# Placing the queries of 16 attention units with stride-one columns, and copying the first layer's result on one engine

## The chip, the cores and the metric

The kernel runs on one core of a Trainium2 chip. The metric is device time in microseconds (us). TensorE (PE, with its weight loads as PEld) multiplies, VectorE (DVE), ScalarE (ACT) and GpSimd (POOL) do elementwise work, SyncE (SP) issues every DMA of this kernel, in one queue.

## What is computed

Chunked local attention, then two feed-forward layers. Four batches, eight heads, 768 positions, head size 64. For each chunk of 32 queries the keys are 8 memory keys and the window from 16 positions before the chunk to 8 behind it, 64 in all where the sequence doesn't cut it:

```python
scores = scale * np.matmul(q_c, k_full.transpose(0, 1, 3, 2))
a = softmax(scores)                       # over the 64 keys
out[:, :, c_start:c_end] = np.matmul(a, v_full)
...
x = out as (3072, 512)                    # heads side by side
x = leaky_relu(x @ w_in, 0.01) @ w_out    # 512 -> 2048 -> 512
return (x @ w_a) * (x @ w_b) @ w_out2     # 512 -> 1536 -> 512
```

All inputs and outputs are float32.

## The kernel before

The 3072 tokens form six blocks of 512 (`bi` 0 to 5); each block is four attention units of 128 tokens, so there are 24 units. While TensorE works on the first feed-forward layer of block `bi`, the attention of block `bi + 1` is put between its steps. A step `f` of a block is one of the 16 slices of the layer's 2048 hidden columns: `mm1` (12 matmuls, lines 303 to 305) into a PSUM bank, a Prelu by ScalarE (line 383), a rounding copy by ScalarE (`gh`, line 320), a subtraction (`gl`, line 321), and two steps later `mm2` (12 matmuls, lines 398 to 402) into the four accumulators `acc[bi][e]` of the block. At a block's end the accumulators are copied to SBUF tiles `x2` (lines 410 and 412) and written to DRAM (line 413). The four PSUM buffers `a` of the accumulators are the same for all blocks, so the next block's first `mm2` waits for these copies. The tiles `x2` share three buffers (tag `z`).

Unit `u` of block `bi + 1` is spread over the steps of block `bi`: scores at step `f` (2, 5, 8, 11; in block 0 5, 8, 11, 14), softmax at `f` and `f + 1`, transposes by VectorE at `f + 2`, the product with the values (`a_pv`, line 276) and its copy out (`a_out`) at `f + 3`.

The scores of a unit are 16 products of 128x64 weights, the queries, with 64 columns of keys (line 202); in the trace they are 32 weight loads and 32 matmuls. The 64 query columns hold two heads: partitions 0 to 63 hold one head in columns 0 to 31 and zeros in the others, partitions 64 to 127 the other head in columns 32 to 63. The tile is laid out `[partition, column, o]` with 16 products `o`, so the 64 columns of one product lie 16 floats apart. Two such tiles `Q` are used in turn; the zeros are written once at the start (lines 158 to 160), and two DMAs for each unit write the queries into their halves (lines 173 and 174). `load_qk(u)` loads the queries up to unit `u + 2`, right behind the scores of `u`.

The values of `a_pv` are weights of the same 128x64 shape, `v[:, i:i + 64]`, with their columns next to each other.

In blocks 0 to 4 ScalarE, VectorE and GpSimd also prepare the weights of the later layer (`prep_steps`, lines 471 to 515): load raw words, join, round, subtract, store. ScalarE and VectorE execute in the order that the planner of the language gave them. After the last block the second layer runs (lines 660 to 741).

Of the kernel before, what the change touches and what calls it, by code (L numbers as in the profile page):

```python
# [7 lines left out]
F32 = mybir.dt.float32  # L8
# [6 lines left out]
P = 128  # L15
B, H, S, D = 4, 8, 768, 64
CH, LEFT, RIGHT, NMEM = 32, 16, 8, 8
# [3 lines left out]
NU = B * UPB  # L21
# [10 lines left out]
def kernel(  # L32
# [10 lines left out]
    nc = tc.nc  # L43
# [11 lines left out]
    tp = ctx.enter_context(tc.tile_pool(name="tp", bufs=4, side="right"))  # L55
# [96 lines left out]
    Q = [ap_.tile([P, 2 * CH, 16], F32, tag=f"q{i}", name=f"q{i}", bufs=1) for i in range(2)]  # L152
# [16 lines left out]
    def q_load(upto):  # L169
        while loaded[0] < min(upto, NU):  # L170
            u = loaded[0]
            qb = Q[u % 2]
            nc.sync.dma_start(out=qb[0:64, 0:CH, :], in_=q_l[u, 0:64])
            nc.sync.dma_start(out=qb[64:128, CH:2 * CH, :], in_=q_l[u, 64:128])
            loaded[0] += 1

    def k_load(upto):
        while loaded[1] < min(upto, 2 * NU):
            u, cp = divmod(loaded[1], 2)
            t = ap_.tile([P, 512], F32, tag="k", name="k")  # L180
            nc.sync.dma_start(out=t, in_=k_l[u, cp])
            kt[u, cp] = t
            loaded[1] += 1
# [8 lines left out]

    def a_scores(u):
        qb = Q[u % 2]
        s = ps_s.tile([P, 8, 64], F32, tag="s", name="s")
        for cp in range(2):
            k = kt.pop((u, cp))
            for hp in range(4):
                for cpar in range(2):
                    o = (2 * cp + cpar) * 4 + hp  # L200
                    r = (cpar * 4 + hp) * 64
                    nc.tensor.matmul(  # L202
                        s[64 * cpar:64 * cpar + 64, cp * 4 + hp, :],
                        qb[:, :, o],
                        k[:, r:r + 64],
                        start=True, stop=True,
                    )
        st[u] = s
# [123 lines left out]

    x_tiles(("x", 0))
    q_load(1)
    k_load(2)
    q_load(2)
    k_load(4)
    nc.sync.dma_start(out=ident, in_=id_l)
    v_load(4)
    W1.load(1)  # L340
    k1 = kt[1, 1]
    a_scores(0)
    a_scores(1)

    warm = ps_a.tile([P, TB], F32, tag="a", name="warm")
    with tc.high_priority(offset=-100000):
        for _ in range(8):
            nc.tensor.matmul(
                warm[:, 0:128], k1[:, 0:128], k1[:, 0:128], start=True, stop=True
            )  # L350
    q_load(4)
    k_load(8)
    W1.load(4)
# [14 lines left out]
    W1.split(1, nc.vector)  # L368
    a_out(1, ("x", 0), UT)
    a_scores(2)  # L370
    a_soft1(2)

# [13 lines left out]
    def mm2(bi, parts, g):  # L386
        if bi not in acc:
            acc[bi] = [ps_a.tile([P, TB], F32, tag="a", name="a") for _ in range(KC)]
        gh, gl = g
        for o, n, f in parts:  # L390
            slot = wslot[f, 1]
            t = slice(o, o + n)
            for e in range(KC):
                ps = acc[bi][e][:, t]
                c = slice(e * P, e * P + P)

                kw = dict(skip_group_check=n < TB)
                nc.tensor.matmul(  # L398
                    ps, slot[:, 1, c], gh[:, t], start=f == 0 and o == 0, stop=False, **kw
                )  # L400
                nc.tensor.matmul(ps, slot[:, 0, c], gl[:, t], start=False, stop=False, **kw)  # L401
                nc.tensor.matmul(  # L402
                    ps, slot[:, 0, c], gh[:, t], start=False, stop=f == NF1 - 1, **kw
                )
            if f == NF1 - 1:
                for e in range(KC):
                    ps = acc[bi][e][:, t]
                    y = tp.tile([P, TB], F32, tag="z", name="x2", bufs=3)
                    if e % 2:
                        nc.vector.tensor_copy(y[:, t], ps)  # L410
                    else:
                        nc.scalar.copy(y[:, t], ps)
                    nc.sync.dma_start(out=x2d[bi][:, e, t], in_=y[:, t])

    HALF, LEAD = TB // 2, 3
# [12 lines left out]
    def at(bi, f, fn, *args):  # L428
        beside.setdefault((bi, f), []).append(lambda: fn(*args))
# [22 lines left out]
    for bi in range(NB3 - 1):  # L452
        for k, f in enumerate([5, 8, 11, 14] if bi == 0 else [2, 5, 8, 11]):
            u = (bi + 1) * (TB // UT) + k
            at(bi, f, a_scores, u)
            at(bi, f, load_qk, u)
            at(bi, f, a_soft1, u)
            at(bi, f + 1, a_soft2, u)
            at(bi, f + 2, a_turn, u)
            at(bi, f + 3, a_pv, u, ps_s, "s")  # L460
            at(bi, f + 3, load_v, u)
            at(bi, f + 3, a_out, u, ("x", bi + 1), k * UT)
# [125 lines left out]
    for n, (bi, f, parts) in enumerate(items):  # L588
# [16 lines left out]
        if len(behind) > LAG:  # L605
            mm2(*behind.pop(0))
# [31 lines left out]
    for it in behind:  # L638
        mm2(*it)
# [191 lines left out]
```

## Time and profile before

| | us |
|---|---|
| median of three runs | 1192.63 (1191.24 to 1194.59) |
| profiled execution | 1194.71 |
| its span, first to last instruction | 1192.9 |
| TensorE matmul busy | 1158.3 (97%) |
| TensorE weight loads busy | 974.7 (82%) |
| VectorE busy | 681.2 (57%) |
| ScalarE busy | 383.2 (32%) |
| GpSimd busy | 109.6 (9%) |

Busy times are those of the engine's own instructions. Weight loads run beside matmuls. A busy TensorE may still be paced by its weight loads, since matmuls overlap each other in the records.

### The profile page before, as it was taken

To read this page: it belongs to the slowest core of one execution; us is meant where nothing else is said; L and a number is where in the kernel's file an instruction comes from. 1 tells how busy PE (TensorE), PEld (TensorE's weight loads), DVE (VectorE), ACT (ScalarE), POOL (GpSimd) and SP (SyncE) were. 2 spreads that over 40 slices of the span, in tenths; PEclk is the share of its full clock that TensorE was granted. 3 is DMA by queue.
4 is the path that set the end of the run, shared out by engine and by line. 5 is a ranking of instruction groups with operands and counts; after the bars stand their busy time and mean duration, and the time that the engine had idled before them with its cause. 6 is when DMAs were issued, how large, how long until landed. Compare 5 with 4: busy or idle time off the path is not lost.

```text
span 1192.9 us, 16632 instructions
## 1 busy us (share of the span) xinstructions
PE 1158.3 (97%) x6632; PEld 974.7 (82%) x6632; DVE 681.2 (57%) x1246; ACT 383.2 (32%) x642; POOL 109.6 (9%) x77
## 2 busy tenths in 40 slices
PE   5799999999998999999999999999999999999998
PEld 4799988878886888888888888888888888888887
DVE  5979876978768694644511543457433456433444
ACT  3735343444334343223422222233122233122210
POOL 1421211231222230000000000000000000000000
PEclk9899999999998999999999999999999999999999
DMA  9867788879697887434435733537453535453512
GB/s 333 295 220 246 248 293 298 310 268 321 253 337 254 292 297 258 142 107 159 159 106 220 265 124 124 194 124 291 159 203 124 194 124 220 159 203 124 194 62 106
DMA packets 63821, 250.71 MB, mean 210 GB/s; under 512 B 7424, under 2 KB 8832, under 8 KB 56832
## 3 DMA queue, kind: packets, MB, share of 16 engines
q1 hardware_dynamic: 63744, 249.66, 58.8%
q8 instruction: 52, 0.85, 0.3%
q14 instruction: 25, 0.20, 0.0%
HBM read 200.34 MB, written 49.28 MB: 209 GB/s over the span
## 4 chain that ended last, share of the span: by engine, by line
PE 81%; DVE 10%; DMA 3%; POOL 2%; issue 2%; ACT 1%; SPq 0%; DVEq 0%; ACTq 0%; POOLq 0%
PE o L727 5%; PE o L729 5%; PE o L728 5%; PE h L303 5%; PE a L398 5%; PE a L401 5%; PE a L402 5%; PE h L304 5%; PE h L305 5%; PE A L660 4%; PE A L662 4%; PE A L661 4%; PE C L660 3%; PE C L662 3%; PE C L661 3%; PE s L202 3%
## 5 line engine op out<-in xcount | busy, mean ns | idle before, releaser
L303 PE MATMUL h<-xh,w 128*128 128x512 f32 (+1 forms) x448 | 165.2, 369 | 5.5 <-DVE w L94 5.5
L398 PE MATMUL a<-gh,w 128*128 128x512 f32 (+1 forms) x448 | 162.4, 362 | 8.3 <-DVE x L410 7.1
L401 PE MATMUL a<-gl,w 128*128 128x512 f32 (+1 forms) x448 | 161.9, 361 | 5.3 <-POOL gl L321 5.3
L304 PE MATMUL h<-xl,w 128*128 128x512 f32 (+1 forms) x448 | 161.8, 361 | 0.0
L305 PE MATMUL h<-xh,w 128*128 128x512 f32 (+1 forms) x448 | 161.7, 361 | 0.0
L402 PE MATMUL a<-gh,w 128*128 128x512 f32 (+1 forms) x448 | 161.6, 361 | 0.0
L321 DVE TENSOR_TENSOR gl<-g,gh 128x512 fp32r<-128x512 f32 x80 | 61.9, 776 | 102.2 <-ACT gh L320 101.5
L727 PE MATMUL o<-w,cl 128*128 128x512 f32 x288 | 112.1, 389 | 0.0
L729 PE MATMUL o<-w,ch 128*128 128x512 f32 x288 | 112.0, 389 | 0.0
L728 PE MATMUL o<-w,ch 128*128 128x512 f32 x288 | 112.0, 389 | 0.0
L383 ACT ACTIVATE g<-h 128x512 f32<-128x512 f32 (+1 forms) x99 | 57.5, 580 | 157.1 <-PE h L305 157.1
L398 PEld LDWEIGHTS a<-gh,w 128*128 128x128 f32 x448 | 85.4, 191 | 23.0 <-DVE x L410 8.6
L303 PEld LDWEIGHTS h<-xh,w 128*128 128x128 f32 x448 | 85.1, 190 | 19.5 <-issue 5.8
L401 PEld LDWEIGHTS a<-gl,w 128*128 128x128 f32 x448 | 85.5, 191 | 18.0 <-POOL gl L321 5.5
L246 DVE STREAM_TRANSPOSE pt<-p 32x128 f32<-32x128 f32 x320 | 96.8, 302 | 5.3
L402 PEld LDWEIGHTS a<-gh,w 128*128 128x128 f32 x448 | 85.6, 191 | 12.6
L305 PEld LDWEIGHTS h<-xh,w 128*128 128x128 f32 x448 | 85.1, 190 | 13.0
L304 PEld LDWEIGHTS h<-xl,w 128*128 128x128 f32 x448 | 85.3, 190 | 12.0
L674 ACT COPY u<-A 128x512 f32<-128x512 f32 x72 | 42.3, 587 | 143.6 <-PE A L662 143.6
L682 DVE TENSOR_TENSOR ga<-u,C 128x512 f32<-128x512 f32 x36 | 24.8, 688 | 105.1 <-ACT u L674 75.9
L660 PE MATMUL A<-ch,wab 128*128 128x512 f32 x216 | 84.1, 389 | 0.0
L661 PE MATMUL A<-cl,wab 128*128 128x512 f32 x216 | 84.1, 389 | 0.0
(94 smaller groups left out, 1970.7 us busy)
## 6 DMA issues: line engine op xcount, KB each, us to landing
wab<-wab SPq DMA_DIRECT2D x36, 1792.0 KB, 7.3
w<-wod SPq DMA_DIRECT2D x116, 512.0 KB, 4.7
raw<-w SPq DMA_DIRECT2D x68, 512.0 KB, 6.3
wab<-pw SPq DMA_DIRECT2D x12, 1792.0 KB, 6.8
k<-kl SPq DMA_DIRECT2D x48, 256.0 KB, 4.9
v<-vl SPq DMA_DIRECT2D x48, 256.0 KB, 5.2
wod<-w SPq DMA_DIRECT2D x16, 512.0 KB, 5.5
q<-ql SPq DMA_DIRECT2D x48, 128.0 KB, 5.1
```

The costliest lines, as they stand in the source:

```text
L246: nc.vector.transpose(out=pt[o0:o0 + 32, :, 2 * cpar + hpar, hpx, :], in_=p[i0:i0 + 32, hpx::2, 32 * b:32 * b + 32],)
L303: nc.tensor.matmul(ps, w[1], x[0], start=first, stop=False)
L304: nc.tensor.matmul(ps, w[0], x[1], start=False, stop=False)
L305: nc.tensor.matmul(ps, w[0], x[0], start=False, stop=last)
L398: nc.tensor.matmul(ps, slot[:, 1, c], gh[:, t], start=f == 0 and o == 0, stop=False, **kw)
L401: nc.tensor.matmul(ps, slot[:, 0, c], gl[:, t], start=False, stop=False, **kw)
L402: nc.tensor.matmul(ps, slot[:, 0, c], gh[:, t], start=False, stop=f == NF1 - 1, **kw)
L660: nc.tensor.matmul(ps, w[:, 1, i, c], hi[:, kc], start=first and kc == 0, stop=False, **kw)
L661: nc.tensor.matmul(ps, w[:, 0, i, c], lo[:, kc], start=False, stop=False, **kw)
L727: nc.tensor.matmul(o, cl[:, q], w[:, 0, :], start=k == 0, stop=False)
L728: nc.tensor.matmul(o, ch[:, q], w[:, 1, :], start=False, stop=False)
L729: nc.tensor.matmul(o, ch[:, q], w[:, 0, :], start=False, stop=k == NCH - 1)
```

## The change

From unit 8 on, the queries no longer go by DMA into their places. One DMA for each unit brings them as they are into a tile of the pool `tp` (tag `t`, four buffers, shared with the Prelu's output `g`). Three steps after the scores of unit `u`, `q_place(u + 2)` lets ScalarE copy the two halves into the same buffer `Q`, now read as `[partition, o, column]`, so that the 64 columns of a product are next to each other. The copy reads with a step of 16 floats. For units 8 and 9 GpSimd first writes the zeros of the new layout. The scores of units 8 to 23 read the new layout. Units 0 to 7 are as before. Besides, all copies of `x2` out of the accumulators are made by ScalarE; VectorE made every second one.

```diff
     def q_load(upto):
         while loaded[0] < min(upto, NU):
             u = loaded[0]
-            qb = Q[u % 2]
-            nc.sync.dma_start(out=qb[0:64, 0:CH, :], in_=q_l[u, 0:64])
-            nc.sync.dma_start(out=qb[64:128, CH:2 * CH, :], in_=q_l[u, 64:128])
+            if u < QB:
+                qb = Q[u % 2]
+                nc.sync.dma_start(out=qb[0:64, 0:CH, :], in_=q_l[u, 0:64])
+                nc.sync.dma_start(out=qb[64:128, CH:2 * CH, :], in_=q_l[u, 64:128])
+            else:
+                t = tp.tile([P, CH, 16], F32, tag="t", name="qr")
+                nc.sync.dma_start(out=t, in_=q_l[u])
+                qr[u] = t
             loaded[0] += 1
+
+    qr = {}
+    QB = 8
+
+    def q_place(u):
+
+        if not QB <= u < NU:
+            return
+        t = qr.pop(u)
+        qb = Q[u % 2].rearrange("p c o -> p (c o)").rearrange("p (o c) -> p o c", c=2 * CH)
+        if u < QB + 2:
+            nc.gpsimd.memset(qb[0:64, :, CH:2 * CH], 0.0)
+            nc.gpsimd.memset(qb[64:128, :, 0:CH], 0.0)
+        for h in range(2):
+            p = slice(64 * h, 64 * h + 64)
+            nc.scalar.copy(
+                qb[p, :, CH * h:CH * h + CH], t[p].rearrange("p c o -> p o c")
+            )
...
     def a_scores(u):
         qb = Q[u % 2]
+        if u >= QB:
+            qb = qb.rearrange("p c o -> p (c o)").rearrange("p (o c) -> p c o", c=2 * CH)
...
-                    if e % 2:
-                        nc.vector.tensor_copy(y[:, t], ps)
-                    else:
-                        nc.scalar.copy(y[:, t], ps)
+                    nc.scalar.copy(y[:, t], ps)
                     nc.sync.dma_start(out=x2d[bi][:, e, t], in_=y[:, t])
...
             at(bi, f + 1, a_soft2, u)
+            at(bi, f + 3, q_place, u + 2)
             at(bi, f + 2, a_turn, u)
```

## Rows read from the trace of the kernel before

**Rows 1.** Busy time of each engine by stretches (us from the span's start): length, then PE, PEld, DVE, ACT and POOL, each with its instructions; the granted clock, the DMA share and GB/s stand at the end.

```profile
0.00:150.00 150.00, 125.98 (x1290) 121.49 (x1291) 121.84 (x255) 71.51 (x129) 36.13 (x28) 0.95 0.79 267
150.00:480.00 330.00, 322.90 (x2043) 266.77 (x2042) 245.92 (x501) 130.97 (x222) 73.50 (x49) 0.99 0.82 289
480.00:660.00 180.00, 180.00 (x972) 149.22 (x971) 68.69 (x135) 48.95 (x78) 0.00 (x0) 1.00 0.44 150
```

**Rows 2.** Groups of instructions by line and shape, the scores (L202) and the product with the values (L276): count, busy us, mean ns of one, idle time before.

```profile
L202 PE MATMUL s<-k,q 128*64 128x64 f32 x768 | 47.7, 281 | 6.5 <-DMA k<-kl 6.5
L202 PEld LDWEIGHTS s<-k,q 128*64 128x64 f32 x768 | 45.0, 204 | 8.7 <-issue 8.3
...
L276 PE MATMUL pv<-pt,v 128*64 128x64 f32 x768 | 30.0, 229 | 4.2 <-DVE pt L246 2.8 <-issue 1.4
L276 PEld LDWEIGHTS pv<-pt,v 128*64 128x64 f32 x768 | 26.0, 141 | 11.8 <-issue 7.4 <-DVE pt L246 3.4 <-ACT pt L262 0.3
```

**Rows 3.** TensorE's matmuls in order of time around one unit's values and the next unit's scores: start, us from the first start to the last end, instruction, count.

```profile
411.62 0.39 PE L402 MATMUL a<-gh,w 128*128 128x512 f32 x1
411.94 1.15 PE L276 MATMUL pv<-pt,v 128*64 128x64 f32 x32
412.92 1.94 PE L202 MATMUL s<-k,q 128*64 128x64 f32 x32
414.79 0.50 PE L303 MATMUL h<-xh,w 128*128 128x512 f32 x1
```

**Rows 4.** Groups by line and shape: copies of 64 partitions by ScalarE, the copies of x2 by either engine, the zeros by GpSimd.

```profile
L410 DVE COPY x<-a 128x512 f32<-128x512 f32 x10 | 6.9, 687 | 8.4 <-PE a L402 4.8 <-DMA x2d<-x 3.6
...
L412 ACT COPY x<-a 128x512 f32<-128x512 f32 x10 | 5.6, 586 | 5.9 <-PE a L402 5.9
...
L262 ACT COPY pt<-pT 64x512 f32<-64x512 f32 x4 | 2.3, 582 | 0.0
...
L412 ACT COPY x<-a 128x256 f32<-128x256 f32 x4 | 1.5, 374 | 0.0
...
L159 POOL MEMSET q<- 64x512 f32 x2 | 1.0, 517 | 0.3 <-POOLq L813 0.3
```

**Rows 5.** Who waited for whom: us in total, times, the longest.

```profile
ACT raw L79 <- DMA raw<-w: 30.7, 14, 6.8
...
ACT pw L93 <- DMA wab<-pw: 20.3, 7, 6.7
...
PE a L398 <- DVE x L410: 7.1, 4, 3.3
...
DVE x L410 <- DMA x2d<-x: 4.2, 4, 1.7
```

**Rows 6.** TensorE in order of time: the matmuls that waited for copies of x2, with the idle time and its releaser in brackets.

```profile
144.41 0.39 PE L398 MATMUL a<-gh,w 128*128 128x256 f32 x1 [0.74 <-DVE x L410]
...
264.93 0.50 PE L398 MATMUL a<-gh,w 128*128 128x512 f32 x1 [1.51 <-DVE x L410]
...
363.97 0.50 PE L398 MATMUL a<-gh,w 128*128 128x512 f32 x1 [0.39 <-ACT x L412]
...
367.10 0.51 PE L398 MATMUL a<-gh,w 128*128 128x512 f32 x1 [1.48 <-DVE x L410]
...
371.42 0.79 PE L398 MATMUL a<-gh,w 128*128 128x512 f32 x1 [3.35 <-DVE x L410]
```

**Rows 7.** The stretches around the longest of these waits, with the columns of rows 1.

```profile
365.00:370.00 5.00, 1.60 (x6) 0.68 (x4) 4.84 (x9) 1.48 (x3) 2.59 (x2) 1.00 0.82 265
370.00:377.00 7.00, 5.58 (x40) 4.34 (x41) 6.90 (x11) 2.15 (x4) 2.37 (x1) 0.52 0.53 190
377.00:390.00 13.00, 13.00 (x59) 10.75 (x58) 10.03 (x26) 4.95 (x9) 3.70 (x3) 1.00 0.76 277
```

**Rows 8.** ScalarE in order of time at the ends of blocks 1 and 2: its copies of x2 and its next rounding of the later layer's weights.

```profile
258.26 1.06 ACT L412 COPY x<-a 128x512 f32<-128x512 f32 x2
...
264.31 1.05 ACT L93 CAST pw<-ps 128x1024 fp32r<-128x1024 f32 x1 [1.08 <-DVE ps L491]
...
363.33 1.07 ACT L412 COPY x<-a 128x512 f32<-128x512 f32 x2
...
369.55 1.05 ACT L93 CAST pw<-ps 128x1024 fp32r<-128x1024 f32 x1 [3.27 <-DVE ps L491]
```

**Rows 9.** VectorE in order of time: its copies of x2 at the ends of blocks 2 and 5.

```profile
366.36 0.68 DVE L410 COPY x<-a 128x512 f32<-128x512 f32 x1
...
370.68 0.68 DVE L410 COPY x<-a 128x512 f32<-128x512 f32 x1
...
654.84 0.69 DVE L410 COPY x<-a 128x512 f32<-128x512 f32 x1 [1.43 <-DMA x2d<-x]
```

**Rows 10.** SyncE's queue behind the scores that start at 324.13: the two DMAs of the queries.

```profile
329.37 1.23 SPq L173 DMA_DIRECT2D q<-ql  x1
330.65 1.31 SPq L174 DMA_DIRECT2D q<-ql  x1
```

**Rows 11.** DMA issues by line: count, KB each, median us to landing.

```profile
q<-ql SPq DMA_DIRECT2D x48, 128.0 KB, 5.1
...
x2d<-x SPq DMA_DIRECT2D x20, 256.0 KB, 3.5
```

**Rows 12.** TensorE in order of time three steps behind the same scores: the first matmul of that step's `mm1` and the first of the `mm2` behind it.

```profile
324.13 1.94 PE L202 MATMUL s<-k,q 128*64 128x64 f32 x32
...
337.04 0.39 PE L303 MATMUL h<-xh,w 128*128 128x512 f32 x1
...
339.76 0.39 PE L398 MATMUL a<-gh,w 128*128 128x512 f32 x1
```

## The prediction

> **What bounds the kernel now.** I read the busy times by stretches first, to see where TensorE is the limit. The 16 changed units do their scores while blocks 1 to 4 run, about 150 to 560 us. In 150 to 480 us TensorE is busy 322.9 of 330 us, in 480 to 660 us 180 of 180 [rows 1]. VectorE has 246 of 330 us, ScalarE 131, the DMA engines a share of 0.82. So in this part a microsecond taken from TensorE's stream is a microsecond of the kernel, and half a microsecond more of ScalarE is hidden as long as nothing on TensorE waits for it. Before 150 us it is different: VectorE has 122 of 150 us and TensorE 126 [rows 1]; but of the new scores none lies there.
>
> Second, the groups by line. The scores and the product with the values are the same shape, 128x64 weights against 64 columns, 768 of each, but a weight load takes 204 ns in one and 141 in the other, a matmul 281 and 229 [rows 2]. What differs in the operands is the weights' layout: queries 16 floats apart, values side by side. Third, TensorE in order of time: the 32 matmuls of one unit's values are followed directly by the 32 of the next unit's scores. From first start to first start the values take 0.98 us, the scores 1.87; from end to end (411.62 + 0.39 = 412.01, 413.09, 414.86) 1.08 and 1.77 [rows 3].
>
> Last, what TensorE does wait for in the middle: only the copies of x2 at block ends, 0.74, 1.51, 0.39, 1.48 and 3.35 us, together 7.5 [rows 6]. After the longest, the granted clock is 0.52 in 370 to 377 us [rows 7], close to the 1.2 GHz level; TensorE had idled from 365 to 371 but for 0.9 us. The 5.58 us busy there would have been some 2.7 us shorter at 2.4 GHz (5.58 x 0.48).
>
> **The scores.** For units 8 to 23 I take the pace of the values. The gain of a unit is 0.69 us by ends (1.77 - 1.08) and 0.89 by starts (1.87 - 0.98); the truth lies between, since neighbouring instructions overlap differently. I take the middle, 0.79: 16 x 0.79 = 12.6 us, with 11.0 to 14.2 as bounds. Below that, the bound is nothing, if the layout isn't the reason (a rival).
>
> What the row shows is that 64 columns load in 204 ns in one layout and in 141 in the other [rows 2]. The Trainium skill (TensorE: Matmul & The Clock Gate, section LDWEIGHTS) says that a weight load's time follows from its number of columns alone; by that, 64 columns cost the same in any layout, and the scores would gain nothing. The trace disagrees, as far as no other difference between the two lines explains 63 ns. The Trainium skill (Advanced Engine Details and Errata, section Memory Cachelines) says that SBUF reads pay when each access goes to another 16-byte line, which steps of 64 bytes always do; the trace agrees with the sign.
>
> **Placing the queries.** Two ScalarE copies of 64 partitions x 512 for each unit. The nearest row is 582 ns, with a contiguous read [rows 4]. The strided read isn't in the trace; the nearest price is that of the strided weights, 63 ns on 64 columns, so 0.5 us on 512 elements. Between 0.58 and 1.1 us each, 32 of them, are 19 to 35 us of ScalarE; I take the lower end for the engine's load, since the copy goes element by element anyway, but nothing in the sum depends on it. What hides it: a step's `mm1` and `mm2` take 2.7 us each (337.04 to 339.76) [rows 12], and a Prelu's result is needed four such groups after its `mm1`, 10.9 us, while Prelu, rounding and subtraction take about 2 us. Slack is therefore some 8.9 us. ScalarE is already held up to 6.8 us by late DMAs [rows 5] without TensorE stopping outside block ends [rows 6]. Placed behind the Prelu of the third step, the copies find ScalarE with 131 of 330 us busy. Cost on the path: 0; if the cover is gone, see the last rival.
>
> The load has to be there earlier: before, it was needed six steps behind the scores, now three. The two issues behind the scores at 324.13 come at 329.37 and 330.65 [rows 10], land 5.1 us later [rows 11], so by about 336 to 337; the step's `mm1` ends at 339.76 [rows 12], and its Prelu and rounding come first. There are some 4 us to spare. In SP's queue one issue replaces two, and its wait for the scores of `u` becomes one for a free buffer of `t`; the loads of keys behind it wait for those scores anyway. I count nothing for it. The raw queries hold one of four buffers that the Prelu uses too, leaving three for a tile that lives about 2 us in a step of 5.4: nothing. GpSimd's four memsets of 0.52 us [rows 4] fall at the end of block 0, where it has 36 of 150 us busy [rows 1]: nothing.
>
> **The copies of x2.** 14 copies move: 10 of 512 columns and 4 of 256. VectorE loses 10 x 0.69 plus four of less, about 8.5 us; ScalarE gains 10 x 0.59 + 4 x 0.37 = 7.4 us [rows 4]. Only block ends can feel this. At the end of block 2 ScalarE did its two copies at 363.33 and VectorE's two came at 366.36 and 370.68, behind its own backlog [rows 8, 9]. Four copies in a row on ScalarE would end near 365.7 if none had to wait. The first three then are in time, and the 1.48 us at 367.10 vanish. The fourth needs the first one's buffer, so its DMA, 3.5 us from issue to landing [rows 11]: not before some 368. And ScalarE itself has a rounding in its queue that waits for VectorE until 369.55 [rows 8]; if the planner puts the fourth copy behind it, it ends at 371.2, as late as before. The same choice at the end of block 1: before that rounding at 264.31 the 1.51 us vanish, behind it the copy ends near 266 and the wait grows by about a microsecond. At the end of block 5 the fourth copy waited for its buffer until 654.84 [rows 9]; on ScalarE it may hold a copy out of the second layer's accumulator, worth at most 0.7 us by that row (655.4 + 0.6 against a need near 655.3). Bounds: all waits vanish and the clock stays up, -10.2 us (7.5 + 2.7); or the ends of blocks 1 and 3 each get the worst wait of before with its low clock, 6.05 us each less the 1.51 paid now, and no other gain, +10.6. I take -2: the third copy's wait of 1.48 goes, and the rest half and half.
>
> **The sum.** 1194.7 (the profiled execution) - 12.6 - 2.0 = 1180.1. The profiled execution is 2.1 us above the median of the runs, so the median should be 1192.6 - 14.6 = 1178.0.
>
> **Rivals.** (a) Block ends clear up altogether: 1192.6 - 12.6 - 10.2 = 1169.8. For it: two of the five waits are VectorE's backlog and nothing else. Against: the fourth copy's buffer. (b) Block ends get worse: the fourth copy is put behind a waiting rounding, and ScalarE's later Prelus behind it: 1192.6 - 12.6 + 4 to 10.6, 1184 to 1190.6. For it: ScalarE's waits for VectorE and DMA [rows 5, 8]. Against: at the end of block 5 the planner kept a late copy from blocking VectorE. (c) The layout isn't what makes the scores slow; the change there does nothing, and block ends give 0 to 4: 1188.6 to 1192.6, likeliest 1190.6, no measurable change. For it: the two lines also differ in their moving operand and output. Against: those are contiguous reads in both, and the difference sits in the weight loads, 63 ns, not only in the matmuls. By the Trainium skill's section on LDWEIGHTS this would be the outcome. (d) Slower: the placement waits for a late load in ScalarE's queue, on top of a hold of 6.8 us [rows 5]; 6.8 + 5.1 exceeds the slack of 8.9 by 3.0, TensorE stops for that and pays 2.7 of low clock, 5.7 for each unit hit. It eats the gain of 14.6 from the third unit on; with four units hit the time is 1178.0 + 22.8 = 1200.8. Against: 4 us to spare where I looked, and it must coincide with the longest holds.
>
> **How the numbers follow.** Forecast 0.60, (a) 0.14, (b) 0.14, (c) 0.07, (d) 0.05. About 0.3% (3.6 us) is what a measurement here tells from no change, so faster means under 1189.0. That holds for the forecast, (a), nearly all of (b) and a little of (c): 0.88. Same: most of (c), a little of (b): 0.07. Slower: (d), 0.05. The range takes in all of the forecast (1174 to 1183), most of (a) and the larger part of (b): 1169 to 1188.
>
> **What would show it.** Right: the weight loads of the scores near 141 ns for 16 of 24 units, TensorE's stretch from the first score to the next `mm1` near 1.0 to 1.2 us, no idle TensorE at steps with a placement, copies of about 0.58 to 1.1 us, and TensorE still above 97% busy. Wrong: loads that stay at 204 ns; new idle times of TensorE before line 398 at block ends, or before line 401 where a subtraction comes late; a granted clock near 0.5 behind them.

## The result and the profile after

The changed kernel takes 1206.84 us (median of four runs, 1205.79 to 1207.15). The kernel before, on the same chip, took 1191.93 (1190.17 to 1194.59). The ratio is 1.0114, with a 95% interval of 1.0089 to 1.0140: slower, on the other side of no change than forecast (1178.0, range 1169 to 1188). The profiled execution took 1205.79 us, its span is 1204.0, the mean granted clock 0.980 (before: 0.991).

The stretches of [rows 1] and the groups of [rows 2, 4], now of the changed kernel. Line 227 is the scores, 301 the product with the values, 196 the placement.

```profile
0.00:150.00 150.00, 121.80 (x1204) 117.45 (x1205) 122.31 (x252) 73.39 (x126) 36.94 (x31) 0.92 0.76 260
150.00:480.00 330.00, 314.50 (x2040) 258.41 (x2039) 235.97 (x486) 155.37 (x251) 73.09 (x50) 0.96 0.79 283
480.00:660.00 180.00, 180.00 (x1010) 148.79 (x1010) 67.78 (x135) 58.13 (x90) 0.00 (x0) 1.00 0.43 149
```

```profile
L227 PE MATMUL s<-k,q 128*64 128x64 f32 x768 | 36.7, 255 | 6.4 <-DMA k<-kl 6.4
L196 ACT COPY q<-qr 64x512 f32<-64x512 f32 x32 | 34.9, 1092 | 10.0 <-PE s L227 5.8 <-DMA qr<-ql 4.0
L227 PEld LDWEIGHTS s<-k,q 128*64 128x64 f32 x768 | 33.9, 169 | 8.9 <-issue 8.5
...
L301 PEld LDWEIGHTS pv<-pt,v 128*64 128x64 f32 x768 | 27.2, 144 | 18.6 <-issue 10.6 <-DVE pt L271 7.2 <-ACT pt L287 0.3
```

The scores did become cheaper. Group means mix 8 units of the old layout with 16 of the new: 169 ns = (204 + 2 x 151) / 3, so a load of the new layout takes some 151 ns in the mean instead of 204. The median is 138, and the mean is higher because single loads take up to 232 ns: in `e3_own_buffer` (below), whose granted clock is 1.00 from 200 to 560 us where it is 0.97 here, the same loads take 138 at most. TensorE in order of time around one unit (values, scores, next `mm1`), against [rows 3]:

```profile
427.91 1.15 PE L301 MATMUL pv<-pt,v 128*64 128x64 f32 x32
428.89 1.10 PE L227 MATMUL s<-k,q 128*64 128x64 f32 x32
429.93 0.50 PE L328 MATMUL h<-xh,w 128*128 128x512 f32 x1
```

From the first score to the next `mm1` 1.04 us now, 1.87 before. What is new is that TensorE stops. TensorE in order of time, its longest idle times behind the first 60 us of the changed kernel, with their releaser:

```profile
123.79 0.30 PE L301 MATMUL pv<-pt,v 128*64 128x64 f32 x2 [2.99 <-issue]
...
131.67 0.39 PE L328 MATMUL h<-xh,w 128*128 128x256 f32 x1 [2.48 <-ACT g L408]
...
173.66 0.79 PE L423 MATMUL a<-gh,w 128*128 128x512 f32 x1 [2.49 <-ACT x L434]
...
232.30 0.33 PE L301 MATMUL pv<-pt,v 128*64 128x64 f32 x2 [1.36 <-DVE pt L271]
...
280.59 0.80 PE L423 MATMUL a<-gh,w 128*128 128x512 f32 x1 [4.41 <-ACT x L434]
...
368.55 0.79 PE L329 MATMUL h<-xl,w 128*128 128x512 f32 x1 [2.26 <-DVE xl L315]
390.75 0.50 PE L423 MATMUL a<-gh,w 128*128 128x512 f32 x1 [2.15 <-ACT x L434]
```

It waits for Prelus, for copies of `x2`, for the turned softmax and for the next block's input: not one late thing, but several that ScalarE and VectorE hand to it. Around the stops the granted clock is lower, 0.57 to 0.83 in the six stretches of 7 to 15 us that hold them. Two of these, with the columns of rows 1, and then the whole part from 120 to 450 us:

```profile
120.00:135.00 15.00, 8.47 (x89) 7.83 (x88) 14.69 (x34) 7.28 (x13) 3.45 (x4) 0.80 0.54 202
...
278.00:285.00 7.00, 4.41 (x37) 3.46 (x38) 1.47 (x3) 3.08 (x5) 3.86 (x3) 0.57 0.98 361
...
120.00:450.00 330.00, 307.97 (x2091) 256.54 (x2090) 248.36 (x514) 159.97 (x259) 79.04 (x56) 0.95 0.80 289
```

In the kernel before the same stretch, 120 to 450 us, had TensorE busy for 321.19 us at a clock of 0.99. So 13.2 us more of idleness, and about 0.04 x 308 = 12 us for the lower clock (an estimate from these rows), stand against some 10 us that the scores of 12 units gave back. That is 15 us, and the scores of unit 20, the first after this stretch, start at 488.8 instead of 473.9 us.

The start of the scores of a unit is a good ruler for where time goes. From TensorE in order of time (us; `u6` is unit 6, the kernels below the second row are those of the experiments):

| kernel | u6 | u8 | u12 | u16 | u19 | u20 | u23 |
|---|---|---|---|---|---|---|---|
| before | 106.5 | 163.7 | 265.8 | 373.0 | 432.3 | 473.9 | 532.2 |
| after | 107.0 | 175.2 | 282.2 | 387.0 | 448.0 | 488.8 | 544.5 |
| e1_queries_only | 105.6 | 170.2 | 277.1 | 381.7 | 443.1 | 483.9 | 539.6 |
| e3_own_buffer | 106.8 | 165.5 | 262.2 | 370.2 | 425.9 | 466.7 | 522.4 |
| e12_other_queue | 106.9 | 165.8 | 278.6 | 385.6 | 443.6 | 484.2 | 540.0 |
| e6_from_unit_12 | 106.5 | 162.7 | 265.2 | 370.7 | 433.0 | 475.4 | 531.1 |
| e15_own_buffer_from_12 | 107.0 | 163.2 | 264.6 | 361.4 | 422.9 | 463.9 | 519.6 |

In block 4 nothing stops TensorE. Three units take 58.3 us before and 55.7 after: 0.87 us for each unit, 13.9 for sixteen. The loss comes earlier. Between the scores of units 6 and 8, at the end of block 0 and before the first new score, the changed kernel falls 11 us behind. Up to unit 12 it falls another 5 us behind, though four new scores should have given back 3.5; from unit 12 to unit 20 it gains 1.5 us, where eight should have given 7.

### The profile page after: what moved, and what is told of

It reads as the page before. It is cut to its first block, busy times and chain, and to the rows that moved or that the text cites. A ratio compares the mean times of both kernels' runs of the same rounds, so it can differ in the third digit from the quotient of the medians.

```text
span 1204.0 us, 16689 instructions
## 1 busy us (share of the span) xinstructions
PE 1156.8 (96%) x6632; PEld 971.2 (81%) x6632; DVE 673.1 (56%) x1232; ACT 422.1 (35%) x688; POOL 110.0 (9%) x81
## 4 chain that ended last, share of the span: by engine, by line
PE 64%; DMA 2%; DVE 2%; POOL 1%; ACT 0%; issue 0%; SPq 0%; DVEq 0%; ACTq 0%; POOLq 0%
PE o L751 5%; PE o L752 5%; PE o L750 5%; PE A L684 4%; PE A L685 4%; PE A L683 4%; PE a L423 3%; PE a L426 3%; PE a L427 3%; PE h L328 3%; PE h L330 3%; PE h L329 3%; PE C L683 3%; PE C L684 3%; PE C L685 3%; PE D L684 1%
## 5 line engine op out<-in xcount | busy, mean ns | idle before, releaser
L328 PE MATMUL h<-xh,w 128*128 128x512 f32 (+1 forms) x448 | 167.4, 374 | 8.5 <-DVE w L94 5.5
L329 PE MATMUL h<-xl,w 128*128 128x512 f32 (+1 forms) x448 | 164.5, 367 | 2.3 <-DVE xl L315 2.3
L330 PE MATMUL h<-xh,w 128*128 128x512 f32 (+1 forms) x448 | 164.5, 367 | 0.0
L328 PEld LDWEIGHTS h<-xh,w 128*128 128x128 f32 x448 | 87.1, 195 | 23.3 <-issue 5.7
L330 PEld LDWEIGHTS h<-xh,w 128*128 128x128 f32 x448 | 87.0, 194 | 13.0
L427 PEld LDWEIGHTS a<-gh,w 128*128 128x128 f32 x448 | 86.0, 192 | 12.6
```

Of the source, the lines that this page charges most:

```text
L328: nc.tensor.matmul(ps, w[1], x[0], start=first, stop=False)
L329: nc.tensor.matmul(ps, w[0], x[1], start=False, stop=False)
L330: nc.tensor.matmul(ps, w[0], x[0], start=False, stop=last)
L427: nc.tensor.matmul(ps, slot[:, 0, c], gh[:, t], start=False, stop=f == NF1 - 1, **kw)
```

## The experiments

All medians are of several runs, each beside runs of the kernel before on the same chip. The chips differ from row to row, so two rows are best compared by their ratios.

| kernel | us | before | ratio, 95% |
|---|---|---|---|
| after | 1206.84 | 1191.93 | 1.0114 (1.0089 to 1.0140) |
| e1_queries_only | 1202.39 | 1192.44 | 1.0090 (1.0072 to 1.0108) |
| e2_x2_only | 1193.32 | 1192.44 | 1.0001 (0.9983 to 1.0019) |
| e5_layout_by_host | 1184.56 | 1192.44 | 0.9944 (0.9929 to 0.9959) |
| e11_host_layout_x2_act | 1183.77 | 1192.25 | 0.9931 (0.9913 to 0.9949) |
| e3_own_buffer | 1183.68 | 1192.44 | 0.9937 (0.9916 to 0.9958) |
| e8_own_buffer_x2_before | 1183.88 | 1192.25 | 0.9928 (0.9910 to 0.9946) |
| e6_from_unit_12 | 1192.09 | 1192.25 | 1.0001 (0.9987 to 1.0014) |
| e15_own_buffer_from_12 | 1182.41 | 1193.68 | 0.9912 (0.9880 to 0.9944) |
| e12_other_queue | 1201.63 | 1191.93 | 1.0083 (1.0053 to 1.0112) |
| e18_own_buffer_late_load | 1198.64 | 1192.39 | 1.0058 (1.0039 to 1.0077) |
| e19_one_element_no_wait | 1187.11 | 1192.09 | 0.9961 (0.9946 to 0.9976) |
| e10_contiguous_read | 1181.56 | 1192.25 | 0.9920 (0.9891 to 0.9948) |

**Which of the two parts?** `e1_queries_only` is the changed kernel with the copies of `x2` on two engines as before, `e2_x2_only` the kernel before with these copies on ScalarE.

```diff
-                    nc.scalar.copy(y[:, t], ps)
+                    if e % 2:
+                        nc.vector.tensor_copy(y[:, t], ps)
+                    else:
+                        nc.scalar.copy(y[:, t], ps)
```

> The change with the copies of x2 left as they were (every second one by VectorE). Theory 1: the loss has two sources, about 7.5 us at the end of block 0, where the planner put two Preludes of the first layer (Prelu, ScalarE) behind a copy that waits for TensorE, and the rest at block ends, where the fourth copy of x2 stands behind a rounding that waits for a store of 1.8 MB. Here only the first stays, and 16 units gain 0.85 us each: 1192 + 7.5 - 13.6 = 1186, between 1181 and 1191. Rival 2: the strided placements, 1.09 us each instead of 0.58, hold ScalarE so that every later stall follows from them: then no better than 1200. Rival 3: any new order of the planner costs some 10 us whatever it is: 1195 to 1207.

> The kernel before with all copies of x2 by ScalarE, nothing else. Theory 1: the fourth copy is late at block ends, at three of them by 2 to 4.5 us, each followed by some 3 us of low clock: 1192 + 5 to 14, likeliest 1200. Rival 2 (strided placements are the cause): 1192, no change. Rival 3: 1195 to 1207.

The queries alone cost 10 us, the copies alone nothing that can be told. Both miss what I thought likeliest, 1186 and 1200. With both, the time is 4.4 us above that of the queries alone, 2.9 by the ratios, whose intervals overlap. The ruler shows a difference too: between units 6 and 8 `e1` loses 7.4 us where the changed kernel loses 11, and it doesn't have the stop for a copy of `x2` at 173.66.

**Is it the layout?** In `e5_layout_by_host` all 24 units get the new layout ready in DRAM, zeros included, and one DMA per unit writes it into `Q`. There is no placement, and the host does the rearrangement. `e11_host_layout_x2_act` is the same with the copies of `x2` on ScalarE.

```diff
-            nc.sync.dma_start(out=qb[0:64, 0:CH, :], in_=q_l[u, 0:64])
-            nc.sync.dma_start(out=qb[64:128, CH:2 * CH, :], in_=q_l[u, 64:128])
+            nc.sync.dma_start(out=Q[u % 2], in_=q_l[u])
...
-                        qb[:, :, o],
+                        qb[:, o, :],
```

> The kernel before, but the host lays the queries of all 24 units out as the scores' weights want them, zeros included (512 KB for each unit instead of 256), and one DMA for each unit brings them: no placement, no sharing of buffers, no memsets, x2 as before. Theory 1: the weight loads fall to the values' 140 ns, 18 units in the part that TensorE paces gain 0.8 us each, the first few nothing: 1192 - 14 = 1178, between 1172 and 1184, if the larger DMAs hide. If stride is not what makes the scores slow: 1192. If the 6 MB more of queries cost DMA time: 1185 to 1195.

> Queries of all units laid out by the host with their zeros, no placement, and the copies of x2 by ScalarE alone. The former gave 1184.6 with x2 as before, and its longest wait of TensorE was 3.3 us for VectorE's copy of x2. If ScalarE alone makes that copy in time: 1178 to 1182. If it is late there too, as alone in the kernel before (5.6 us at one block end): 1183 to 1187.

With all 24 units in the new layout the loads of the scores take:

```profile
L197 PEld LDWEIGHTS s<-k,q 128*64 128x64 f32 x768 | 28.5, 154 | 8.7 <-DMA q<-ql 6.5 <-issue 1.7 <-DMA wod<-w 0.2
```

154 ns in the mean (the median is 138), against 204 [rows 2], and the kernel is 0.56% faster, a little less than I had expected (1178, at most 1184). So the layout is what made the scores slow, and the loss is in how the queries get into it. With the copies of `x2` on ScalarE (`e11`) the time is the same.

**The shared buffers.** `e3_own_buffer` is the changed kernel with the raw queries in a tag of their own, one buffer, and three buffers left for the Prelu (and for the copies of the second layer that use the same tag, not shown): the same memory, split. `e8_own_buffer_x2_before` is that with the copies of `x2` as before.

```diff
-                t = tp.tile([P, CH, 16], F32, tag="t", name="qr")
+                t = tp.tile([P, CH, 16], F32, tag="qr", name="qr", bufs=1)
...
-        g = tp.tile([P, TB], F32, tag="t", name="g")
+        g = tp.tile([P, TB], F32, tag="t", name="g", bufs=3)
...
```

> The whole change, but the raw queries have a tile tag of their own with one buffer, and the Prelu's output three instead of four shared ones (same memory). Theory 1: the Prelus of steps 12 and 13 of block 0 no longer stand behind the copy of the values' product, TensorE's 6.4 us of idle time in 120 to 132 us and the low clock behind it go: 1206.8 - 7.5 = 1199, between 1195 and 1202; block ends are as bad as in the changed kernel. Rivals 2 and 3: 1204 to 1210.

> Raw queries with a buffer of their own, copies of x2 by both engines as before. If the copies of x2 by ScalarE alone are worth nothing either way, as alone in the kernel before: 1183.7, between 1181 and 1187. If they help where placements load ScalarE: 1187 to 1192. If they hurt there: 1177 to 1181.

1183.68: a split of the same four buffers is worth 23 us by the medians, 21 by the ratios, far more than I had expected (1199). The placement (32 copies of 1098 ns), its DMAs and three buffers for the Prelu are all still there; only the sharing is gone. Here the loads of the scores show their price without the low clock, 160 = (204 + 2 x 138) / 3:

```profile
L227 PEld LDWEIGHTS s<-k,q 128*64 128x64 f32 x768 | 31.7, 160 | 8.6 <-issue 8.3
```

`e8` gives the same time, so the copies of `x2` are worth nothing here either.

**Block 0 and the later blocks.** `e6_from_unit_12` is the changed kernel with the new layout from unit 12 on, so that no raw load or placement lies in block 0; `e15_own_buffer_from_12` is `e3` with the same edit.

```diff
-    QB = 8
+    QB = 12
```

> The changed kernel, buffers shared with the Prelu's output as there, but placements start at unit 12 instead of 8, so the first raw load falls into block 1. Theory 1, sharpened by the runs so far: the sharing is the whole loss, and it bites in block 0, where the queue of DMAs is long and the planner holds the Preludes' output buffers (Prelu) behind the raw load of unit 8; from block 1 on it is harmless: 1192.4 - 12 x 0.8 = 1183, between 1178 and 1188. Rival 4: the sharing costs in every block, by later block ends and late products with the values: about 1206.8 - 10 (block 0) + 3 (four units less) = 1199, between 1194 and 1203.

> The new layout from unit 12 on only, and the raw queries in a buffer of their own. It differs from e6_from_unit_12 (1192.1 us) by the buffer alone, and has no placement in block 0. Theory: sharing the buffers costs in block 0 (about 10 us up to the scores of unit 8) and again in blocks 1 to 4; then the 12 units give 12 x 0.85 = 10 us less up to 1.5 us of the third of the placements that is not there, so 1183 to 1187, 5 to 9 us below e6. Rival: sharing costs only in block 0, and e6 lost its gain to something else (the mixed layouts, the start of the placements in block 1); then the time is that of e6, 1190 to 1193.

`e6` lies between the two times that I had expected for it (1183 and 1199). `e15` is 9.7 us below `e6`: sharing costs in blocks 1 to 4 too, and the other 13 of the 23 us come with units 8 to 11, whose first loads and placements lie in block 0. `e15` gains 11.3 us on the kernel before; 12 units at 0.87 are 10.4.

An example of how the two kernels part is unit 17, in block 2; its load is the latest of the twelve of `e6`, counted from the scores before it. SyncE in order of time, first `e6` (shared), then `e15` (own buffer). Both load the raw queries of unit 17. Their place in `Q` is free once the scores of unit 15, which start at 321.9 and 320.3 us, are done:

```profile
314.57 0.33 SPq L607 DMA_DIRECT2D w<-wod  x1
325.28 0.33 SPq L528 DMA_DIRECT2D wab<-pw  x1
325.70 1.35 SPq L212 DMA_DIRECT2D v<-vl  x2
327.10 1.24 SPq L178 DMA_DIRECT2D qr<-ql  x1
```

```profile
306.15 0.33 SPq L178 DMA_DIRECT2D qr<-ql  x1
...
321.44 0.33 SPq L528 DMA_DIRECT2D wab<-pw  x1
```

With its own buffer the load goes at 306.15 us, once the placement before it, which starts at 303.9, has read the buffer. With shared buffers it stands behind a store of the later layer's weights (`wab`) that waits for its data, and is issued 21 us later. ScalarE in the same stretch, again `e6` first:

```profile
331.10 0.63 ACT L245 ACTIVATE p<-p 128x512 f32<-128x512 f32 x1 [5.72 <-DVE p L242]
...
332.99 0.59 ACT L408 ACTIVATE g<-h 128x512 f32<-128x512 f32 x1
...
335.09 2.20 ACT L196 COPY q<-qr 64x512 f32<-64x512 f32 x2
337.31 0.60 ACT L408 ACTIVATE g<-h 128x512 f32<-128x512 f32 x1
...
338.47 0.59 ACT L408 ACTIVATE g<-h 128x512 f32<-128x512 f32 x1
```

```profile
321.49 2.24 ACT L196 COPY q<-qr 64x512 f32<-64x512 f32 x2
327.39 0.63 ACT L245 ACTIVATE p<-p 128x512 f32<-128x512 f32 x1 [3.66 <-DVE p L242]
...
328.86 0.59 ACT L408 ACTIVATE g<-h 128x512 f32<-128x512 f32 x1
...
331.12 0.59 ACT L408 ACTIVATE g<-h 128x512 f32<-128x512 f32 x1
```

In `e15` the placement comes right behind the scores, when ScalarE waits anyway. In `e6` it comes 13 us behind them, between Prelus that are already late, and TensorE then waits for the subtraction behind such a Prelu:

```profile
340.19 0.50 PE L426 MATMUL a<-gl,w 128*128 128x512 f32 x1 [3.03 <-DVE gl L346]
```

**SyncE's queue.** In `e12_other_queue` ScalarE itself issues the raw load; the buffers are shared as in the changed kernel.

```diff
-                nc.sync.dma_start(out=t, in_=q_l[u])
+                nc.scalar.dma_start(out=t, in_=q_l[u])
```

> The changed kernel in everything, buffers shared with the Prelu's output (Prelu) and x2 by ScalarE, but the raw queries are loaded by DMAs that ScalarE issues instead of SyncE. Theory 1, in its present form: buffers of a tag are handed out in program order, so the output of the next Prelu gets its buffer only when the raw load before it has its turn in SyncE's queue, behind loads and stores that wait; the load's place in that queue, not the buffer it takes, makes the Preludes late. In the other queue the load has its turn at once: the Prelus of block 0 come at their time and the run is like that with the buffer of its own, 1184, between 1181 and 1189. Rival 5: the buffer itself is what lacks, three for the Prelu instead of four: 1200 to 1207, as in the changed kernel.

The time goes back by 5 us only. That is within what I had expected if the Prelu lacked a buffer (1200 to 1207); but `e3` gives the Prelu three and is fast, so three are not too few. And the loss in block 0 is gone: the scores of unit 8 start at 165.8 us, as in `e3`. What happens there shows on ScalarE in order of time, from 103 to 133 us: the changed kernel, the kernel before (from 114 us) and `e12` (from 116).

```profile
103.14 0.58 ACT L408 ACTIVATE g<-h 128x512 f32<-128x512 f32 x1
...
129.22 0.59 ACT L314 CAST xh<-pv 128x512 fp32r<-128x512 f32 x1 [5.23 <-PE pv L301]
...
131.02 1.08 ACT L408 ACTIVATE g<-h 128x512 f32<-128x512 f32 x2
```

```profile
114.93 0.58 ACT L383 ACTIVATE g<-h 128x512 f32<-128x512 f32 x1
...
120.12 0.59 ACT L383 ACTIVATE g<-h 128x512 f32<-128x512 f32 x1
...
123.64 0.58 ACT L383 ACTIVATE g<-h 128x512 f32<-128x512 f32 x1
...
132.01 0.58 ACT L289 CAST xh<-pv 128x512 fp32r<-128x512 f32 x1
```

```profile
116.69 0.58 ACT L408 ACTIVATE g<-h 128x512 f32<-128x512 f32 x1
...
121.45 0.59 ACT L408 ACTIVATE g<-h 128x512 f32<-128x512 f32 x1
...
124.96 0.58 ACT L408 ACTIVATE g<-h 128x512 f32<-128x512 f32 x1
```

Before, three Prelus run ahead of the rounding `xh` of the values of unit 6. In the changed kernel no Prelu runs from 103.14 us until that rounding, which waits 5.23 us for TensorE, is done; then come two at once. TensorE meanwhile has no result of a Prelu to work on, and is busy for 8.47 us of the 15 from 120 to 135. Either a buffer of the raw queries' own or another queue for their load brings the old order back.

The raw load itself is not later there than with its own buffer. SyncE's load of unit 8 and ScalarE's placement of it, the changed kernel first, then `e3`:

```profile
118.23 1.12 SPq L178 DMA_DIRECT2D qr<-ql  x1
133.54 2.23 ACT L196 COPY q<-qr 64x512 f32<-64x512 f32 x2
```

```profile
117.94 1.22 SPq L178 DMA_DIRECT2D qr<-ql  x1
132.69 2.22 ACT L196 COPY q<-qr 64x512 f32<-64x512 f32 x2
```

So what is lost here is not lost to a late load, but to Prelus that were put late into ScalarE's order, and it takes both the shared buffers and SyncE's queue. `e12` still loses in the later blocks: with ScalarE issuing it, the load leaves a median 4.9 us before its placement.

**Is it the late load?** From SyncE's issue to the start of the placement, the median over the units is 7.9 us in the changed kernel (3.3 to 15.3), 7.2 in `e6`, 15.7 in `e3` and 17.9 in `e15`. `e18_own_buffer_late_load` makes the load of `e3` late: VectorE writes one element of the raw buffer first, out of the turned softmax that the values just ahead of the scores need. `e19_one_element_no_wait` is its control, the same write of a constant.

```diff
                 t = tp.tile([P, CH, 16], F32, tag="qr", name="qr", bufs=1)
+                nc.vector.tensor_copy(t[0:1, 0, 0:1], PT[(u + 1) % 2][0:1, 0, 0, 0, 0:1])
                 nc.sync.dma_start(out=t, in_=q_l[u])
```

```diff
+                nc.vector.memset(t[0:1, 0, 0:1], 0.0)
```

> e3_own_buffer (1183.7 us) with one change: before each raw load VectorE writes one element of the raw buffer out of the turned softmax of the unit before (the weights of the values that come right before the scores), so that the load can no longer go as soon as the placement before has freed its buffer, but only about when the scores of its own unit start. In e3 the load is issued a median 15.7 us ahead of its placement, in the changed kernel 7.9 us. Nothing else is shared. Theory 1: it is the late load that costs; then the placements wait again, TensorE stops again around block ends and the time goes back more than half of the 23 us, to 1196 to 1208. Theory 2: what costs is that Prelus and raw queries take turns in the same four buffers (a Prelu needs a buffer that only the placement frees); the late load by itself is covered by the 19 us of a unit, and the time stays at 1182 to 1188.

> The control to e18_own_buffer_late_load (1198.6 us): VectorE writes the same one element of the raw buffer before each load, but a constant, so that it needs nothing but the buffer freed by the placement before; it still stands in VectorE's queue. If in e18 the late load costs, this one follows its own lead: with a median lead of load before placement near the 15.7 us of e3 it gives 1182 to 1188; with a lead that is again under 10 us, because VectorE itself comes late, 1192 to 1202. If it was the extra instruction on VectorE that cost in e18, it gives about 1198 with the lead of e3.

The median lead is 9.2 us and the time 1198.64 us (1196.63 to 1200.55) in `e18`; 15.8 us and 1187.11 us (1184.60 to 1188.74) in the control, which lies 3.4 us above `e3` itself. So, with nothing shared, `e18` loses 11.5 us against its control. The loads of units 8 and 9 keep the leads of `e3` (14.7 and 4.6 us), so it says nothing on block 0; from unit 8 to unit 23 sharing costs 12.4 us by the ruler, the changed kernel against `e3`. One thing it doesn't separate. SyncE's own waits in front of the raw load (us in total, times, longest), `e18` first, then the control:

```profile
SPq L179 <- DVE qr L178: 79.3, 12, 11.6
```

```profile
SPq L179 <- DVE qr L178: 29.4, 9, 5.7
```

In `e18` the held load also holds what is behind it in SyncE's queue, 79.3 us in all; in the changed kernel SyncE waits for the raw buffer 1.0 us in all, since its load is late by its place in the order, not by a wait. Which of the two, the late raw queries or the held queue, cost the 11.5 us is open.

**The best version.** `e10_contiguous_read` is `e3` with the raw queries of units 8 to 23 ordered by the host as `[o, column]`, so that the placement reads side by side.

```diff
-                qb[p, :, CH * h:CH * h + CH], t[p].rearrange("p c o -> p o c")
+                qb[p, :, CH * h:CH * h + CH], t[p]
...
+    ql[8:] = np.ascontiguousarray(ql[8:].transpose(0, 1, 3, 2)).reshape(NU - 8, P, CH, 16)
```

> As with the buffer of its own and x2 by ScalarE, but the host lays the queries of units 8 to 23 out so that the placement reads them contiguously. If the length of the placements matters (rival 2, weakened): they fall from 1.09 to 0.58 us, 16 us less of ScalarE, and the time falls below 1183.7 by 2 to 6, 1178 to 1181. Theory 1: ScalarE's time is hidden, 1183.7 within 2.5.

Groups by line and shape, the placement of `e3`, then of `e10`:

```profile
L196 ACT COPY q<-qr 64x512 f32<-64x512 f32 x32 | 35.1, 1098 | 5.9 <-PE s L227 5.0 <-DMA qr<-ql 0.7
```

```profile
L198 ACT COPY q<-qr 64x512 f32<-64x512 f32 x32 | 19.7, 617 | 6.8 <-PE s L229 4.4 <-DMA qr<-ql 2.2
```

15.4 us less of ScalarE bring 2.1 us by the medians, within the intervals: once the load is early, ScalarE's work is hidden. With shared buffers this was not tried. At 1181.56 it is the lowest median here and beats both kernels; `e15` and `e3` can't be told from it.

## Why the prediction was wrong

**What hides ScalarE's extra work.** I argued from busy shares that it costs nothing. Of the work itself that holds once the load is early: `e10` takes 15.4 us of it away and gains next to nothing. But a busy share says what waits now, not what a new order of the same instructions makes wait, and that is what came.

**The scores: right.** I took 0.79 us for a unit; measured are 0.87, and 13.9 for sixteen against 12.6. The loads fell to 138 ns at the full clock (I had said near 141). Rival (c), that the layout isn't the cause, fell with `e5`. The rule of the Trainium skill (TensorE: Matmul & The Clock Gate, section LDWEIGHTS), by which only the number of columns counts, doesn't hold here: the same 64 columns take 204 ns in one layout and 138 in the other.

**The placement's own cost: the upper bound.** I took 0.58 us for a copy, with 1.1 as the upper bound; it is 1.09. I had said that nothing in the sum depends on it, and with a buffer of its own `e10` bears that out.

**The step that failed** is a pair of terms put at nothing. The first is "The raw queries hold one of four buffers that the Prelu uses too, leaving three for a tile that lives about 2 us in a step of 5.4: nothing". It counted buffers, and three are indeed enough for the Prelu: `e3` has three. But the sharing alone costs 23 us by the medians. Some 9 of them lie in block 0 (the ruler from unit 6 to unit 8, the changed kernel against `e3`), where no Prelu runs for 28 us, and the rest lies in the later blocks.

The second is "There are some 4 us to spare ... I count nothing for it". I had the load go 5 us behind the scores [rows 10] and the placement run three steps, some 13 us, behind them. In the changed kernel, from unit 10 on, the placement starts 1.1 to 5.5 us behind the scores, and the load goes between 7.4 us before them and 0.2 behind. Over all units the load leaves a median 7.9 us ahead of its placement, 3.3 at worst, and lands 5.3 us later in the median, so 2.6 us are to spare and at worst none. With its own buffer the load of these units goes 10 us or more before the scores. What I missed is that sharing a buffer changes when instructions are issued, the Prelus in block 0 and the loads in the later blocks.

Even with a buffer of its own (`e3`) the change gives 8.8 us by the medians, not the 13.9 of the scores; where the rest goes is not shown.

**The copies of x2: mechanism seen, sum wrong.** I took -2; measured is nothing in three surroundings (`e2`, `e8` against `e3`, `e11` against `e5`), and with the shared buffers (the changed kernel against `e1`) a loss of 4.4 us by the medians that the intervals don't settle. Rival (b) did happen: in the changed kernel the fourth copy at the end of block 1 comes behind roundings, of which the first waits 4.58 us for a store:

```profile
276.90 0.92 ACT L93 CAST pw<-pz 128x512 fp32r<-128x512 f32 x2 [4.58 <-DMA wab<-pw]
277.73 1.04 ACT L93 CAST pw<-ps 128x1024 fp32r<-128x1024 f32 x1
279.95 0.59 ACT L434 COPY x<-a 128x512 f32<-128x512 f32 x1 [1.18 <-DMA x2d<-x]
```

That is the 4.41 us of TensorE at 280.59. In all, TensorE's waits for `x2` sum to 9.1 us where they were 7.5 [rows 6], a small part of the loss.

**Rival (d): the right sign and nearly the right time, 1200.8, for 0.05.** The nearness is luck. Its mechanism, a placement that waits for its load in ScalarE's queue, is only a small part: such waits sum to 4.0 us in the changed kernel. I had priced the collision at one unit's slack of 8.9 us and called it rare; in block 0 the order of the Prelus changes instead, which no rival had. Its price for a stop, with the low clock behind it, was of the right kind: by the estimate above about as much went to the clock as to the idleness.

**What stays open.** Why the order that the planner writes puts the Prelus of block 0, and the loads of the later blocks, at a later place when the buffers are shared is not shown; that it does is. Nor is it shown by which steps a late load delays Prelus and softmax in the later blocks. One rival was not tried by itself: that Prelus and raw queries take turns in the same four buffers, so that a Prelu has to come behind a placement, whatever the time of the load. More shared buffers would have tested it. In block 0 GpSimd's zeros of unit 9 waited 17.10 us for the scores in the changed kernel and 4.0 at most in `e3`; that was not tried by itself either.

## What to carry to other kernels

Before a DMA-loaded tile is put into the buffers of a tile that an engine makes, look at what the sharing does to the order, that is, to when the load and the engine's own instructions can be issued, and not only at how many buffers are left: a buffer of its own, in the same memory, was worth 23 us here. A busy share near 100% on one engine doesn't tell how much slack the others have. Price a new stop of that engine at more than its idle time: here 13.2 us of it came with some 12 us, by estimate, of lower clock. When a changed kernel is slower although the changed instructions got faster, line up one repeated event (here the first score of each unit) between the traces: it shows in which stretch the time goes.

## What the hardware showed unexpectedly

A ScalarE copy of 64 x 512 elements takes 617 ns when it reads side by side and 1098 when it reads 64 bytes apart (`e10`, `e3`): 0.94 ns more for each of 512 elements. The price is near that of the strided weights, (204 - 138) / 64 = 1.03 ns for each column (`e3`). The Trainium skill (Advanced Engine Details and Errata, section Memory Cachelines) has reads pay when each goes to another 16-byte line; both numbers agree with it in sign.
